# Tile 1's queries go straight behind the keys on SP's queue, and the values wait for a key transfer

## The chip, the cores and the metric

The kernel runs on one core of a Trainium2 chip. The metric is the device time of one execution in microseconds (us). A profiled execution also shows, per engine, when each instruction ran: PE is the matrix engine (PEld its weight loads), DVE, ACT and POOL are the engines that do element-wise work, and SP only issues DMA transfers. POOL and ACT issue DMA transfers as well. Each issuing engine has a DMA queue of its own: in the trace q0 is POOL's, q1 SP's and q10 ACT's.

## The reference

Attention over pooled keys and values, followed by a mixture of four experts in which every token uses every expert:

```python
# q, k, v: (8 batches, 8 heads, 576 tokens, 64), float32
k_p = k.reshape(B, H, S // 8, 8, D).mean(axis=3)      # 72 pooled keys
v_p = v.reshape(B, H, S // 8, 8, D).mean(axis=3)
scores = scale * np.matmul(q, k_p.transpose(0, 1, 3, 2))
attn = softmax(scores)
x = (attn @ v_p).transpose(0, 2, 1, 3).reshape(4608, 512)
p = domain_probs / (domain_probs.sum(-1, keepdims=True) + 1e-09)
out = sum(p[:, e:e+1] * (np.maximum(x @ w1[e], 0.0) @ w2[e] for e in range(4)))
```

w1 is (4, 512, 1024) and w2 is (4, 1024, 512). Nearly all products are those of the experts.

## The kernel before, in words

The 4608 tokens make 36 tiles of 128, and four tiles make a group. For each of the nine groups and each of the four experts PE computes h = relu(x w1) (`up`, L465, copied out by ACT at L469) and then the four tiles' outputs h w2 (`down`, L503, weighted and summed by DVE at L514 and L518). The attention of the next group is put between these products by a plan of slots that is written out by hand (L548 to L597). This steady part starts with the loop at L795.

The change lies in the part ahead of it (L134 to L207 and L600 to L792), which has to make the first group's x from nothing. Instructions stand on each engine in the order in which the code is written, and each engine works through its own in order. The dependencies between engines become semaphore waits, set when the program is built.

The loads at the start are spread over three queues:

- ACT's queue: the queries of tile 0 (`qf[0]`, L144).
- SP's queue: the first batch's keys as float32 in three transfers (`kf`: the 64 last rows at L147, then two times 256 rows at L149). Later, from inside the loop over key parts, the queries of tile 1 (`load_q0(1, nc.sync)`, L726, issued by L139) and the domain probabilities (`dpr`, L727).
- POOL's queue: first a copy of one element of `qf[0]` (L170), which makes POOL wait until those queries have landed. Behind it, in this order: the first batch's values in three transfers (`vraw[0]`, L81 two times, L85), the first half of `w1[0]` (L119), tile 2's queries, the second half of `w1[0]`, tile 3's queries, `w2[0]` in two halves (L127), `w1[1]`, and all that follows. POOL's transfers convert float32 to bfloat16, apart from the queries of tiles 2 and 3.

A transfer on POOL's queue waits, from the ninth on, for the landing of the one eight places before it.

The work on the engines then goes, from L715 on: idle products on PE (`idle_products`, products of zeros whose result is not used, L626); `split_q(0)` casts tile 0's queries on ACT (L601), `turn_q0` turns them on PE (L609), `take_q0` copies them out on ACT (L617). The loop at L721 takes the keys in three parts, in the order in which they are loaded: `fold_keys0` sums eight rows to one on DVE (L640 two times, L645), `turn_keys0` turns the sums on PE (L652), and a few idle products follow. Between the fold and the turning of the second part stand a memset of one element of `qf[1]` on DVE (L725) and the two SP transfers named above; the transfer into `qf[1]` overwrites that element, so SP waits for the memset, and the memset stands behind the folds on DVE. `take_keys0` copies the turned keys to SBUF in two halves of 64 partitions, both on DVE (L665).

After that come `scores(0)` (PE, L328), `split_q(1)`, `turn_q0(1)` and `take_q0(1)` for tile 1, the maxima, differences and exponentials of tile 0 (DVE L342 and L346, ACT L359), `sum_values0` (PE, L672: eight products for the first two row blocks, which need the first value transfer, and eight for the other three, which need the second and third) with `spread_values0` (DVE, L681), the scores of tile 1, and the rest of tile 0's attention: its transposes and their copy (L402, L403), the sums (L693), the context (L418) and its transposes (L707, L710). The first products with `w1[0]` follow (`up_tile`, L481), which from then on fill PE.

Of the kernel before, what the change touches and what calls it, by code (L numbers as in the profile page):

```python
# [18 lines left out]
def kernel(  # L19
# [10 lines left out]
    nc = tc.nc  # L30
# [3 lines left out]
    P = nc.NUM_PARTITIONS  # L34
# [43 lines left out]
    def load_rows(dst, src, parts=((0, NB - 1),)):  # L78
        rows = src.rearrange("h (j r) d -> (h j) (r d)", r=POOL)
        for i0, i1 in parts:  # L80
            nc.gpsimd.dma_start(  # L81
                out=dst[:, i0:i1, :],
                in_=rows[i0 * P:i1 * P].rearrange("(i p) x -> p i x", p=P),
            )
        nc.gpsimd.dma_start(out=dst[0:TAIL, NB - 1, :], in_=rows[(NB - 1) * P:ROWS])  # L85
# [50 lines left out]
    qf = [raw.tile([P, R, D], F32, name=f"qf{c}") for c in range(TPG)]  # L136

    def load_q0(c, queue):
        queue.dma_start(  # L139
            out=qf[c][:].rearrange("p r d -> p (r d)"),  # L140
            in_=q[0][:, c * P:(c + 1) * P, :].rearrange("h (c r) d -> c h (r d)", r=R),
        )

    load_q0(0, nc.scalar)  # L144
    kf = raw.tile([P, NB, POOL * D], F32, name="kf")
    rows0 = k[0].rearrange("h (j r) d -> (h j) (r d)", r=POOL)
    nc.sync.dma_start(out=kf[0:TAIL, NB - 1, :], in_=rows0[(NB - 1) * P:ROWS])  # L147
    for i in (0, 2):
        nc.sync.dma_start(  # L149
            out=kf[:, i:i + 2, :],  # L150
            in_=rows0[i * P:(i + 2) * P].rearrange("(i p) x -> p i x", p=P),
        )
    dpr = const.tile([NT, P, E], F32, name="dpr")

    still = const.tile([P, G], BF16, name="still")
    nc.vector.memset(still[:], 0.0)  # L156
# [5 lines left out]
    for sign, base in ((1, 0), (-1, SP - 1)):  # L162
        nc.gpsimd.affine_select(
            out=own[:], in_=own[:], compare_op=ALU.is_ge, fill=0.0,
# [2 lines left out]
        )  # L167

    waited = const.tile([1, 1], F32, name="waited")
    nc.gpsimd.tensor_copy(out=waited[:], in_=qf[0][0:1, 0, 0:1])  # L170
    load_rows(vraw[0], v[0], ((0, 2), (2, 4)))
    load_w1(0, lambda: load_q0(2, nc.gpsimd))
    load_q0(3, nc.gpsimd)
# [409 lines left out]
    for g in range(2, NG):  # L583
        for i in range(TPG):
            t = g * TPG + i
# [37 lines left out]
    def idle_products(n):  # L623
        ps = ps_o.tile([P, DM], F32, name="o_ps")
        for _ in range(n):
            nc.tensor.matmul(ps[:], lhsT=still[:, 0:P], rhs=still[:], start=True, stop=True)  # L626
# [8 lines left out]
    def fold_keys0(p1, i0, i1):  # L635
        rows = kraw[0][0:p1, i0:i1]
        src = kf[0:p1, i0:i1]
        for n in (4, 2):
            w = n * D
            nc.vector.tensor_add(  # L640
                out=rows[:, :, 0:w], in0=src[:, :, 0:w], in1=src[:, :, w:2 * w]
            )
            src = rows
        twice = [p1, i1 - i0, 2, D]
        nc.vector.tensor_tensor(  # L645
            out=kpad0[0:p1, i0:i1], in0=rows[:, :, 0:D].unsqueeze(2).to_broadcast(twice),
            in1=rows[:, :, D:2 * D].unsqueeze(2).to_broadcast(twice), op=ALU.add,
        )

    def turn_keys0(p1, i0, i1):  # L650
        for i in range(i0, i1):
            nc.tensor.transpose(  # L652
                kT_ps[:, i, 0:p1], kpad0[0:p1, i].rearrange("p z d -> p (z d)"),
                ident[0:p1, 0:p1],
            )

    def take_keys0():
        for z in range(2):
            dst, src = (
                x[z * D:(z + 1) * D].rearrange("x i p -> x (i p)")[:, 0:ROWS].rearrange(  # L660
                    "x (a y j) -> x a y j", y=2, j=SP
                )[:, :, z]
                for x in (kT[0], kT_ps)
            )
            nc.vector.tensor_copy(out=dst, in_=src)  # L665


    def sum_values0():
# [51 lines left out]
    take_q0(0, turn_q0(0))  # L720
    for part, n in (((TAIL, 4, 5), 3), ((P, 0, 2), 4), ((P, 2, 4), 3)):  # L721
        fold_keys0(*part)
        if part[2] == 2:

            nc.vector.memset(qf[1][0:1, 0, 0:1], 0.0)  # L725
            load_q0(1, nc.sync)  # L726
            nc.sync.dma_start(  # L727
                out=dpr[:], in_=moe_domain_probs.rearrange("(t p) e -> t p e", p=P)
            )
        turn_keys0(*part)  # L730
        idle_products(n)
    take_keys0()
    scores(0)
    split_q(1)
# [60 lines left out]
    for s in range(NSTEP):  # L795
        for slot in range(SLOTS):
            part, i = slot % 3, slot // 3
# [41 lines left out]
```

## Time and profile before

| | |
|---|---|
| median of 3 runs | 553.97 us (553.47 to 554.54) |
| profiled execution | 554.65 us |
| its span, first to last instruction | 552.7 us |
| PE busy | 542.3 us (98%) |
| DVE, ACT, POOL busy | 263.3, 212.7, 70.7 us |
| granted PE clock, mean | 0.993 |
| first product with `w1[0]` (L481) | 22.81 us |
| loop at L795 reached (L465) | 40.7 us |

Times in the profile count from the first instruction of the span. A row of the timeline or of the chain gives start, length, engine, line, what is written and read, and how many instructions it merges. A wait is given with the engine and line that waited and what ended the wait. "DMA to landing" is the time from a transfer's issue to the semaphore that tells that it is complete. A row of the table by windows gives, for each stretch, each engine's busy time with its number of instructions, then the granted PE clock as a share, the busy share of the DMA engines, and GB/s.

### The profile page before, as it was taken

The numbers are of one execution on the slowest core, as the hardware profiler recorded it, in microseconds if no ns is written. First come the engines' busy times: TensorE is split into PE (matmuls) and PEld (weight loads), VectorE is DVE, ScalarE is ACT, GpSimd is POOL, SyncE is SP. The second block draws the span as 40 slices with busy tenths as digits, with TensorE's granted clock in tenths as the row PEclk, the third lists the DMA queues.
The fourth block names the chain that finished last, engine by engine and source line by source line (L and its number), as shares of the span: only waits on it lengthen the run. The fifth ranks groups of instructions, "written<-read, shape, count | busy, mean of one in ns | idle before, by whom it ended". The sixth has DMA issues, their size and how long they took to land.

```text
span 552.7 us, 7479 instructions
## 1 busy us (share of the span) xinstructions
PE 542.3 (98%) x3000; PEld 264.3 (48%) x3000; DVE 263.3 (48%) x458; ACT 212.7 (38%) x356; POOL 70.7 (13%) x120
## 2 busy tenths in 40 slices
PE   6899999999999999999999999999999999999997
PEld 2674554444444444444444444444444444444444
DVE  5572857444744445644463444744474444422223
ACT  1465653333333333333333333333333333333330
POOL 6344001121101110112011100101010000000000
PEclk9799999999999999999999999999999999999999
DMA  9999925455646664356535653335333241011002
GB/s 205 223 203 197 200 33 99 73 78 82 119 85 79 83 105 96 54 83 84 106 52 73 85 117 40 53 40 98 61 53 42 72 77 31 16 44 39 0 1 76
DMA packets 110273, 46.43 MB, mean 84 GB/s; under 512 B 87548, under 2 KB 104764, under 8 KB 110240
## 3 DMA queue, kind: packets, MB, share of 16 engines
q0 software_dynamic: 51040, 21.96, 32.1%
q1 hardware_dynamic: 58912, 23.68, 18.0%
q8 instruction: 23, 0.38, 0.3%
q10 hardware_dynamic: 288, 0.33, 0.3%
q14 instruction: 10, 0.08, 0.0%
HBM read 45.16 MB, written 9.44 MB: 99 GB/s over the span
## 4 chain that ended last, share of the span: by engine, by line
PE 96%; DMA 2%; ACT 1%; DVE 0%; issue 0%; SPq 0%; ACTq 0%
PE o_ps L503 45%; PE h_ps L465 44%; PE x_ps L418 2%; PE sc L328 2%; PE h_ps L481 1%; DMA qf<-in_q_dram 1%; DMA kf<-in_k_dram 1%; PE x_ps L448 1%; PE v_ps L672 0%; PE at_ps L402 0%; PE o_ps L535 0%; ACT attnT L403 0%; PE qT_ps L318 0%; PE o_ps L626 0%; DVE kraw L640 0%; PE qT_ps L609 0%
## 5 line engine op out<-in xcount | busy, mean ns | idle before, releaser
L469 ACT ACTIVATE h_sb<-h_ps 128x512 bf16<-128x512 f32 x280 | 167.1, 597 | 296.2 <-PE h_ps L465 293.8
L465 PE MATMUL h_ps<-xT,w 128*128 128x512 bf16 x1120 | 274.1, 379 | 0.0
L503 PE MATMUL o_ps<-w,h_sb 128*128 128x512 bf16 x1144 | 270.3, 379 | 0.0
L503 PEld LDWEIGHTS <-h_sb 128*128 128x128 bf16 x1144 | 111.5, 98 | 132.7
L518 DVE SCALAR_TENSOR_TENSOR acc<-o_ps,p_sb,acc 128x512 f32<-128x512 f32 x107 | 80.3, 750 | 179.4 <-PE o_ps L503 179.4
L465 PEld LDWEIGHTS <-w 128*128 128x128 bf16 x1120 | 106.0, 98 | 117.1
L514 DVE TENSOR_SCALAR acc<-o_ps,p_sb 128x512 f32<-128x512 f32 x36 | 27.0, 750 | 62.3 <-PE o_ps L503 62.3
L561 POOL COPY gated<-x_sb0of 1x1 bf16<-1x1 bf16 x28 | 7.8, 278 | 369.8 <-DVE x_sb0of L427 369.8
L109 POOL DMA_DIRECT2D qrow<-in_q_dram x36 | 30.5, 847 | 23.7 <-issue 7.7
L342 DVE TENSOR_REDUCE mx<-sc 128x8 f32<-128x576 f32 x36 | 27.2, 756 | 11.5 <-PE sc L328 11.5
L346 DVE TENSOR_TENSOR d_sb<-sc,mx 128x576 f32<-128x576 f32 x36 | 27.3, 757 | 1.2
L427 DVE SCALAR_TENSOR_TENSOR x_sb0of<-x_ps,rs 128x512 bf16<-128x512 f32 (+1 forms) x30 | 20.2, 674 | 12.4 <-PE x_ps L418 11.7
L359 ACT ACTIVATE attn<-d_sb 128x576 bf16<-128x576 f32 x30 | 20.5, 683 | 3.2
L380 DVE TENSOR_REDUCE es<-attn 128x8 f32<-128x576 bf16 x28 | 20.8, 743 | 0.0
L418 PEld LDWEIGHTS <-attnT 128*128 128x128 bf16 (+1 forms) x165 | 12.4, 100 | 7.2 <-issue 1.3
L328 PEld LDWEIGHTS <-qT 128*128 128x128 bf16 (+1 forms) x160 | 11.3, 101 | 8.8 <-issue 2.0
L328 PE MATMUL sc<-kT,qT 128*128 128x144 bf16 (+1 forms) x160 | 15.3, 230 | 0.1
L418 PE MATMUL x_ps<-vbd,attnT 128*128 128x192 bf16 (+5 forms) x165 | 15.2, 231 | 0.0
L626 PE MATMUL o_ps<-still 128*128 128x512 bf16 x31 | 10.6, 473 | 1.3 <-DVE still L156 1.3
L243 DVE TENSOR_TENSOR vraw<-vraw 128x1280 bf16<-128x1280 bf16 (+1 forms) x14 | 9.2, 654 | 0.2
L243 DVE TENSOR_TENSOR kraw<-kraw 128x1280 bf16<-128x1280 bf16 (+1 forms) x14 | 9.0, 640 | 0.2
L481 PE MATMUL h_ps<-xT,w 128*128 128x128 bf16 x128 | 8.3, 219 | 0.3
(88 smaller groups left out, 155.4 us busy)
## 6 DMA issues: line engine op xcount, KB each, us to landing
out_dram<-acc SPq DMA_DIRECT2D x35, 256.0 KB, 2.0
w<-in_moe_w_dram POOLq DMA_DIRECT2D x10, 512.0 KB, 14.3
kraw<-in_k_dram POOLq DMA_DIRECT2D x7, 512.0 KB, 8.0
qrow<-in_q_dram POOLq DMA_DIRECT2D x28, 128.0 KB, 3.8
vraw<-in_v_dram POOLq DMA_DIRECT2D x7, 512.0 KB, 7.5
w<-in_moe_w_dram POOLq DMA_DIRECT2D x3, 1024.0 KB, 16.3
kf<-in_k_dram SPq DMA_DIRECT2D x2, 512.0 KB, 5.4
vraw<-in_v_dram POOLq DMA_DIRECT2D x2, 256.0 KB, 4.8
```

Of the source, the lines that this page charges most:

```text
L109: nc.gpsimd.dma_start(out=qrow[t][at:at + n], in_=q[b][:, tok:tok + n, :].rearrange("h p d -> p h d"),)
L328: nc.tensor.matmul(sc[at:at + n, pair // 2, (pair % 2) * PW:(pair % 2 + 1) * PW], lhsT=qT[t][:, pair, at:at + n], rhs=kT[b][:].rearrange(" ...
L342: nc.vector.reduce_max(out=mxs[t][:], in_=by_head(t), axis=AX.X)
L346: nc.vector.tensor_tensor(out=st[t][:], in0=by_head(t), in1=mxs[t][:].unsqueeze(3).to_broadcast([P, 2, 4, SP]), op=ALU.subtract,)
L359: nc.scalar.activation(out=attn[t % 2][:, 0:ROWS].rearrange("p (h j) -> p h j", j=SP), in_=st[t][:].rearrange("p g h j -> p (g h) j"), fun ...
L380: nc.vector.reduce_sum(out=es[:], in_=e, axis=AX.X)
L418: nc.tensor.matmul(ps[at:at + n, h0 * D:(h0 + c1 - c0) * D], lhsT=attnT[t][:, i, at:at + n], rhs=flat[:, c0 * D:c1 * D], start=(i == 0), s ...
L465: nc.tensor.matmul(ps[:], lhsT=w1_sb[e][:, kc, fb * P:(fb + 1) * P], rhs=xT[g][:, kc, :], start=(kc == 0), stop=(kc == KC - 1),)
L469: nc.scalar.activation(out=hs[s][:, fb, :], in_=ps[:], func=ACT.Relu)
L503: nc.tensor.matmul(ps[:], lhsT=hs[s][:, fb, i * P:(i + 1) * P], rhs=w2_sb[e][:, fb, :], start=(fb == 0), stop=(fb == FB - 1),)
L514: nc.vector.tensor_scalar_mul(out=accs[t][:], in0=ps[:], scalar1=p_sb[:, e, t:t + 1])
L518: nc.vector.scalar_tensor_tensor(out=accs[t][:], in0=ps[:], scalar=p_sb[:, e, t:t + 1], in1=accs[t][:], op0=ALU.mult, op1=ALU.add,)
```

## The change

Four edits. The transfer of tile 1's queries and that of the probabilities are issued on SP right behind the three key transfers, and the memset that they waited for is gone. POOL's copy of one element, ahead of the values, reads an element of the keys' second transfer (`kf`, row block 0) in place of one of tile 0's queries. The two halves of the turned keys are copied one on DVE and one on ACT.

```diff
@@ the loads on SP
             out=kf[:, i:i + 2, :],
             in_=rows0[i * P:(i + 2) * P].rearrange("(i p) x -> p i x", p=P),
         )
+    load_q0(1, nc.sync)
     dpr = const.tile([NT, P, E], F32, name="dpr")
+    nc.sync.dma_start(out=dpr[:], in_=moe_domain_probs.rearrange("(t p) e -> t p e", p=P))
@@ ahead of POOL's loads
     waited = const.tile([1, 1], F32, name="waited")
-    nc.gpsimd.tensor_copy(out=waited[:], in_=qf[0][0:1, 0, 0:1])
+    nc.gpsimd.tensor_copy(out=waited[:], in_=kf[0:1, 0, 0:1])
     load_rows(vraw[0], v[0], ((0, 2), (2, 4)))
@@ take_keys0
-            nc.vector.tensor_copy(out=dst, in_=src)
+            (nc.vector.tensor_copy, nc.scalar.copy)[z](out=dst, in_=src)
@@ the loop over the key parts
         fold_keys0(*part)
-        if part[2] == 2:
-
-            nc.vector.memset(qf[1][0:1, 0, 0:1], 0.0)
-            load_q0(1, nc.sync)
-            nc.sync.dma_start(
-                out=dpr[:], in_=moe_domain_probs.rearrange("(t p) e -> t p e", p=P)
-            )
         turn_keys0(*part)
         idle_products(n)
```

## The prediction

> **What bounds the kernel now.** I read the page first: PE is busy 542.3 of 552.7 us, and only the first two of the 40 slices show less than 9 tenths. From 40.85 us on the windows show PE busy throughout, so whatever this change is worth is decided before that, and a gain made there is kept unless a later load becomes late. Next the chain that ended last, in order of time (start, length, what):
>
> ```profile
> 7.86 0.05 DVE kraw L640
> 7.91 6.82 DMA qf<-in_q_dram
> ...
> 14.81 0.63 ACT qrow L601
> ...
> 15.48 0.64 PE qT_ps L609 x16
> ...
> 16.66 2.13 PE v_ps L672 x16
> 18.80 0.48 PE sc L328 x4
> 19.27 0.43 PE at_ps L402 x5
> ```
>
> The transfer of tile 1's queries sits on it for 6.82 us. The waits of PE and ACT up to 22 us, and SP's own, give its price and its cause:
>
> ```profile
> PE qT_ps L609 <- ACT qrow L601: 4.9, 1, 4.9
> ...
> ACT qrow L601 <- DMA qf<-in_q_dram: 9.2, 2, 7.1
> ...
> SPq L139 <- DVE kraw L640: 6.0, 1, 6.0
> ```
>
> PE stands still from 10.61 to 15.48 (4.88 us), and SP had nothing to issue from 2.52 to 7.91, waiting for the fold and the memset of L725. Then the DMA queues between issue and first packet, 8 to 11.9 us, and from 12 to 14.8 us (packets, MB, share):
>
> ```profile
> q0 software_dynamic: 743, 0.71, 119.9%
> ```
> ```profile
> q0 software_dynamic: 299, 0.46, 75.2%
> q1 hardware_dynamic: 188, 0.33, 37.1%
> ```
>
> In the first stretch SP's queue (q1) moved not one packet although its transfer had been issued at 7.91: it stood behind the POOL queue's (q0) values and weights. Last, the values:
>
> ```profile
> DMA to landing us min/median/max: 4.1/5.1/5.4
> ```
>
> Issued at 5.03, 5.86 and 6.57, they land at 9.1, 11.3 and 11.6: long before PE uses them at 16.45. And the clock, in windows whose edges I put on the clock record's steps (5.77, 12.60, 19.43) and halfway between:
>
> ```profile
> 9.19:12.60 3.41, 1.34 (x9) 0.64 (x9) 2.12 (x4) 0.00 (x0) 3.13 (x6) 1.00 1.18 190
> 12.60:16.01 3.41, 0.53 (x16) 0.51 (x16) 0.00 (x0) 0.62 (x1) 1.09 (x2) 0.50 1.14 263
> 16.01:19.43 3.42, 3.42 (x30) 3.03 (x26) 0.60 (x1) 1.17 (x2) 1.39 (x3) 0.50 1.21 245
> 19.43:22.84 3.41, 2.93 (x28) 1.77 (x27) 3.26 (x9) 1.42 (x4) 1.44 (x2) 1.00 1.23 205
> ```
>
> After the stretch with 1.34 us of PE work (first number in front of a bracket) the clock falls to 0.50, and it comes back only after a full one. So the idle time also slows the values' products behind it.
>
> **The change part by part.** Times are on the scale of the profiled execution.
>
> *Tile 1's queries and the probabilities on SP.* The DVE memset (0.06 us) goes, and with it SP's wait. The two issues (0.61 and 0.62 us) follow the last key issue, 2.5 to 3.8 us; nothing else stands on SP's queue until the transposes at 86 us. Their 0.26 and 0.07 MB go behind the keys. Alone, SP's queue moved 0.28 MB in the 0.80 us from 5.0 to 5.8, so they add 0.75 and 0.21 us to the keys' last packet at about 7.1 to 7.3: done at about 8.1. From last packet to landing took 0.45 to 1.0 us for keys and queries, so tile 1's queries land at 8.4 to 9.0 instead of 14.73. The keys stand ahead on the same queue; I take their landings (6.49, 7.77) as unchanged, with 1.0 us late, all of the new traffic, as the bad end.
>
> *The values' gate.* POOL's one-element copy now waits for the second key transfer (6.49) instead of tile 0's queries (4.86): 1.63 us. Behind it on POOL stand the values, both halves of w1[0], the queries of tiles 2 and 3, w2[0] and all later loads; each is issued up to 1.63 us later. The first value packet came at 6.64, 1.61 us behind its issue, and the first of them took about 0.5 us each until SP's queue was empty at 7.3. Now the first comes at 6.66 + 1.61 = 8.27, with SP's queue empty. The shift of the values is thus between 1.2 (counted from where they ran freely) and 1.63 us: last landing at 12.8 to 13.3. I take 13.0, since the freed DMA engines should return part. For later loads the 0.33 MB no longer come between: from 12 to 14.8 us q0 moved 299 packets, where its 743 in 3.9 us give 533, so 1.2 us were lost there and come back. Their net shift is 0 to 0.4, with 1.63 as the bad end.
>
> *The keys' copy on two engines.* Here the built program shows more than the diff: ACT's copy does not wait for PE but for DVE's semaphore at the value which the first half's copy sets. The two halves run one after the other. Before: 0.62 us for both on DVE from 9.52. Now 0.31, a hand-over of 0.05 (the gaps between DVE, ACT and PE in the chain are 0.02 to 0.06), and ACT's half: its copies took 0.325 at 128x256 and 0.69 at 128x640, so 0.36 at 288. End 10.24 instead of 10.14. Bounds: 0.25 earlier if side by side, 0.2 later with the slower hand-overs. ACT's next piece, the cast of tile 1's queries, also waits behind it, though its data are there at 9.0.
>
> *The sum.* Scores of tile 0 on PE 10.3 to 10.7; cast on ACT 10.26 to 10.88; turning on PE (0.44 as for tile 0) to 11.4; one idle product; the first eight value products (values landed by 10.7) to about 12.15. ACT's copy of the turned queries ends at 12.0; DVE's maxima and differences (0.76 each) end at 12.3, exponentials at 13.0. So PE waits from 12.15 for the last values: 13.05. The eight products with 192 columns took 1.28 of the 2.13 us at clock 0.50, so 0.64 at full: end 13.7 instead of 18.79. From there to the first product with w1[0] it was 4.02 us (22.81); 0.48 and 0.43 of it were scores and transposes at half clock, which take 0.26 and 0.29 at full (25.53 and 24.03 us in the chain): 3.66. That product then starts at 17.36: 5.45 us earlier; with values at 13.3 it is 5.15, at 12.8 it is 5.65, and if they never bound (PE free at 12.15) 6.3.
>
> Whether the weights are there: landings (issue plus time to landing) 15.1 and 18.3 for w1[0] against needs of 17.4 and 20.2 (25.62 before); tile 2's queries 16.2 against 18.1; w2[0] 21.5 and 24.6 against 24.2 and 25.5 (29.66 and 30.93 before). The last has the least cover, 0.9 us. Behind it w1[1] (27.2 against 35.3), the second batch's keys (32.6 against 34.4) and w2[2] (59.4 against 62.7; used at 68.05 before) stay covered. Nothing else moves, so I take 5.4 us. The profiled execution took 554.65 us, 1.95 around its span; less 5.4 it is 549.25. It lies 0.68 above the median 553.97, so for the median: 548.6.
>
> *Two rules beside the rows.* The trace: the clock fell at 12.60, after 2.0 us of idle PE, when the stretch before it held 1.34 us of work. The Trainium skill (TensorE: Matmul & The Clock Gate, "What's actually happening") says that the monitor watches free-running windows of about 3.4 us and gates after an idle one; the window length agrees with the steps here, but this window was not idle. By the rule 0.9 us of waiting could never bring half clock; by the row it could, so the rival below is kept. On the queues the row is the missing 4 us of SP packets. The Trainium skill (DMA: Bandwidth & Descriptors, "Queues, rings and completion order") has each DMA engine alternate between queues packet by packet; by that rule the 128 packets of tile 1's queries, at half of 190 per us from 9.3 on, would have landed by about 11.5 (an estimate), 3 us sooner than they did, and lifting the gate would bring 2.2 us instead of 5.4; the trace does not agree.
>
> **The rivals.**
>
> *Half clock stays.* From 9.19 to 12.60 PE would work about 2.5 us by my sum, between 1.34 (fell) and 2.93 (held), nearer the second. If it falls, the value products cost 0.64 more, scores and transposes 0.36, and one more stretch of sums, context and transposes about 1: gain 3.4, 550.6.
>
> *A weight comes late.* With the whole 1.63 us kept, the second half of w2[0] lands at 26.3 against 25.5: 0.8 lost, 549.4. For it: the DMA queue is full until 60 us. Against: the 1.2 us returned.
>
> *The keys come late,* because SP's queue shares its engines with what stands behind: 1.0 us on keys, gate and values: 549.6. Against: the same queue serves in order in the rows.
>
> *Hidden anyway, no change.* If tile 1's queries still wait until POOL's queue has drained, they land near 14 and PE waits as before: 554. Against: POOL now issues 4 us after SP.
>
> *Slower.* The values are held behind SP's queue as tile 1's queries were behind POOL's: first packet 4.07 us after issue instead of the 1.37 of the first keys, 2.7 lost. If each of the three value transfers lost that in turn, the last lands at 21.1, and the kernel is 2.7 us slower: 556.7. It decides from a landing later than 18.5. Against: before, the first value packets came 1.61 us after issue while SP's queue still ran.
>
> **How the numbers follow.** My forecast (values set the pace, 547.6 to 549.0): 0.62. Still better, to 547.2 (the values never bind and the key copies do run side by side): 0.04. Weight late 0.09, keys late 0.05, half clock 0.12: all faster. Hidden 0.03; slower 0.05. From no change a measurement can tell about 0.2%, 1.1 us. Faster 0.92, same 0.03, slower 0.05. The range from 547.2 to 550.8 reaches over the faster cases; what lies beyond is the last two, and some of the tails.
>
> **What would show it.** SP's four issues and the probabilities' without a pause before 4 us; tile 1's cast on ACT at about 10.3, ended by ACT's own copy and not by a DMA; ACT's key copy starting after DVE's; no 4.9 us wait on PE, but one of about 0.9 before L674's last eight products, ended by the values' DMA; a clock of 1.00 from 12.6 to 19.4; the first product with w1[0] near 17.4, and from there everything of before some 5.4 us sooner. Wrong would be: values landing after 14, half clock after 12.6, or a PE wait for w2[0] near 25.

## The result, and the profile after

The changed kernel takes 549.91 us (median of 6 runs, 549.07 to 550.60) against 554.02 us before (6 runs, 553.46 to 555.63). The ratio is 0.9923 with a 95% interval of 0.9907 to 0.9939: 0.6 to 0.9% faster. The forecast was 548.6, with a range from 547.2 to 550.8. The profiled execution took 549.99 us with a span of 547.9, which is 4.8 us less than the span of before. One run of the kernel with only the new gate (712.42 us, mean clock 0.754) and one of the kernel before beside it (637.78 us, 0.848) were slow ones and are left out of the medians below.

The chain that ended last in the changed kernel, in order of time (start, length, what). Lines behind L155 carry numbers 2 higher than before.

```profile
6.08 0.70 POOL waited L172
6.79 1.49 POOL vraw L81 x2
8.27 5.14 DMA vraw<-in_v_dram
...
13.46 0.83 PE v_ps L674 x8
14.29 0.25 PE sc L330 x4
```

Tile 1's queries are gone from it. In their place stand POOL's gate copy, the issue of the values, and the landing of the last of them. PE's waits up to 22 us say the same:

```profile
PE v_ps L674 <- DMA vraw<-in_v_dram: 1.5, 1, 1.5
...
PE qT_ps L611 <- ACT qrow L603: 0.2, 1, 0.2
```

The wait for the cast of tile 1's queries fell from 4.9 to 0.2 us, and one of 1.5 us for the values came. The timeline shows how each edit came out:

```profile
2.56 0.61 SPq L139 DMA_DIRECT2D qf<-in_q_dram  x1
...
3.21 0.59 SPq L155 DMA_DIRECT2D dpr<-in_moe_domain_probs_dram  x1
...
6.05 0.69 DVE L642 TENSOR_TENSOR kraw<-kf 128x512 bf16<-128x512 f32 x1 [1.56 <-DMA kf<-in_k_dram]
6.08 0.70 POOL L172 COPY waited<-kf 1x1 f32<-1x1 f32 x1 [4.00 <-DMA kf<-in_k_dram]
...
9.33 0.30 DVE L667 COPY kT<-kT_ps 64x288 bf16<-64x288 bf16 x1 [0.38 <-PE kT_ps L654]
...
9.66 0.39 ACT L667 COPY kT<-kT_ps 64x288 bf16<-64x288 bf16 x1 [2.45 <-DVE kT L667]
...
10.08 0.62 ACT L603 CAST qrow<-qf 128x512 bf16<-128x512 f32 x1
...
17.94 1.27 PE L483 MATMUL h_ps<-xT,w 128*128 128x128 bf16 x16
```

SP issues without a pause. Tile 1's queries took 6.2 us from issue to landing and were there at 8.8; their cast follows ACT's own copy and waits for no transfer. The two halves of the keys run one after the other: ACT waited for DVE. The first product with `w1[0]` comes at 17.94 instead of 22.81. From there to the end everything is as long as before: from the loop's first product (L465, now L467) to the end of the span it is 512.0 us in both.

One row shows something new. POOL's copy of one element, 0.18 us before, took 0.70, ending with the DVE instruction beside it.

And the clock stayed at 1.00 from its first step, at 4.85 us, on. Counted from that step, the stretch of 3.41 us that had least PE work in it was this one:

```profile
11.68:15.09 3.41, 1.91 (x24) 1.41 (x21) 1.18 (x3) 1.05 (x3) 2.78 (x4) 1.00 1.17 189
```

### The profile page after: what moved, and what is told of

Read it like the earlier page. It is cut to its first block, busy times and chain, and to the rows that moved or that the text cites. A ratio compares the mean times of both kernels' runs of the same rounds, so it can differ in the third digit from the quotient of the medians.

```text
span 547.9 us, 7477 instructions
## 1 busy us (share of the span) xinstructions
PE 540.3 (99%) x3000; PEld 262.3 (48%) x3000; DVE 262.9 (48%) x456; ACT 213.3 (39%) x357; POOL 71.2 (13%) x120
## 4 chain that ended last, share of the span: by engine, by line
PE 96%; DMA 2%; ACT 1%; POOL 0%; DVE 0%; issue 0%; SPq 0%
PE o_ps L505 45%; PE h_ps L467 44%; PE x_ps L420 2%; PE sc L330 2%; PE h_ps L483 1%; DMA vraw<-in_v_dram 1%; DMA kf<-in_k_dram 1%; PE x_ps L450 1%; PE at_ps L404 0%; PE o_ps L537 0%; POOL vraw L81 0%; ACT attnT L405 0%; PE qT_ps L320 0%; ACT xT L712 0%; PE v_ps L674 0%; POOL waited L172 0%
## 5 line engine op out<-in xcount | busy, mean ns | idle before, releaser
L467 PE MATMUL h_ps<-xT,w 128*128 128x512 bf16 x1120 | 274.2, 379 | 0.0
L467 PEld LDWEIGHTS <-w 128*128 128x128 bf16 x1120 | 105.8, 98 | 117.2
L348 DVE TENSOR_TENSOR d_sb<-sc,mx 128x576 f32<-128x576 f32 x36 | 27.3, 757 | 1.2
## 6 DMA issues: line engine op xcount, KB each, us to landing
w<-in_moe_w_dram POOLq DMA_DIRECT2D x10, 512.0 KB, 14.2
kraw<-in_k_dram POOLq DMA_DIRECT2D x7, 512.0 KB, 6.4
vraw<-in_v_dram POOLq DMA_DIRECT2D x7, 512.0 KB, 5.9
kf<-in_k_dram SPq DMA_DIRECT2D x2, 512.0 KB, 5.0
```

What stands on the lines that cost most here:

```text
L348: nc.vector.tensor_tensor(out=st[t][:], in0=by_head(t), in1=mxs[t][:].unsqueeze(3).to_broadcast([P, 2, 4, SP]), op=ALU.subtract,)
L467: nc.tensor.matmul(ps[:], lhsT=w1_sb[e][:, kc, fb * P:(fb + 1) * P], rhs=xT[g][:, kc, :], start=(kc == 0), stop=(kc == KC - 1),)
```

## The experiments

### How much of the gain is the clock

The kernel before, with PE kept busy during the wait; no transfer is moved.

```diff
     take_keys0()
     scores(0)
+    idle_products(20)
     split_q(1)
```

> The kernel before with 20 more idle products behind the scores of tile 0, some 4.3 us of PE work in the wait for tile 1's queries; no transfer is moved. My theory: the clock stays at 1.00 past 12.6 us, the queries land at 14.7 as before, and what stands behind them up to the first product with w1[0] is 1.0 to 1.5 us shorter; 552.5 to 553.2. The rest of the change's gain is the transfer's. Rival (the clock is most of the gain): 551 or less. Third outcome (the clock falls all the same): 554.0.

Measured: 552.34 us (552.27 to 552.93), ratio 0.9970 (0.9959 to 0.9981). All six runs had a mean clock of 1.000, where 12 runs of the kernel before beside them had 0.994 to 0.997. The chain:

```profile
7.84 7.06 DMA qf<-in_q_dram
...
15.65 0.44 PE qT_ps L609 x14
16.09 0.33 PE o_ps L626
16.41 1.11 PE v_ps L672 x16
```

The transfer still takes 7 us, and landed at 14.89, 0.16 later than before. Behind it the value products take 1.11 us instead of 2.13, and the first product with `w1[0]` comes at 21.17 instead of 22.81. The clock alone is worth 1.9 us by the medians, a little more than the 1.0 to 1.5 expected for it. The rival, that it is most of the gain, falls: 1.9 of 4.1 us.

### The parts of the change one by one

The first run has only the SP edit; the second puts it together with the two-engine copy, without the new gate; the third has the SP edit and the new gate, without the two-engine copy; the fourth has only the new gate.

The changed kernel with the old gate and both copies on DVE, that is, the kernel before with only the SP transfers moved:

```diff
-    nc.gpsimd.tensor_copy(out=waited[:], in_=kf[0:1, 0, 0:1])
+    nc.gpsimd.tensor_copy(out=waited[:], in_=qf[0][0:1, 0, 0:1])
...
-            (nc.vector.tensor_copy, nc.scalar.copy)[z](out=dst, in_=src)
+            nc.vector.tensor_copy(out=dst, in_=src)
```

> The kernel before with only the two SP transfers put behind the keys and the memset gone. My theory: this edit alone carries the gain; it is as fast as the changed kernel with the old gate, 549.1 (548.6 to 549.9). Rival (the three edits are needed together): 550.5 or more.

Measured: 548.75 us (548.53 to 549.52), ratio 0.9901 (0.9886 to 0.9916). Repeated on another occasion:

> Only the two SP transfers moved, once more: 548.4 to 549.5 as before (548.75), clock 1.00 in all runs, third key transfer at about 7.8 us. If it comes out over 549.6, its lead of 1.1 us over the changed kernel was of the occasion.

Measured: 549.02 us (548.41 to 549.34), ratio 0.9905 (0.9891 to 0.9919); the third key transfer landed at 8.3 here, at 7.8 in the first. So the SP edit alone carries the gain and more: its ten runs lie between 548.41 and 549.52, the changed kernel's six between 549.07 and 550.60. By the medians the SP edit alone is 0.9 to 1.2 us below the changed kernel, though measured on other occasions. Its chain has no transfer behind the keys any more:

```profile
2.06 5.71 DMA kf<-in_k_dram
...
7.79 0.70 DVE kraw L642
...
10.19 0.42 PE sc L330 x4
...
10.64 0.77 DVE mx L344
...
11.43 0.77 DVE d_sb L348
...
12.22 0.69 ACT attn L361
```

The values, issued at 4.95, land at 11.63, and the second eight products start at 11.68 with no wait. From the third key part on it is the work itself that follows: fold, scores, maxima, differences, exponentials.

The changed kernel with only the gate put back:

```diff
-    nc.gpsimd.tensor_copy(out=waited[:], in_=kf[0:1, 0, 0:1])
+    nc.gpsimd.tensor_copy(out=waited[:], in_=qf[0][0:1, 0, 0:1])
```

> The changed kernel with the values' gate put back on tile 0's queries. My theory (since the change, the landing of the last values sets the pace, one for one): the values are issued at about 5.0 us and land at 11.6 to 12.3, PE is ready for them at about 12.1, the first product with w1[0] comes at 17.0 to 17.3 instead of 17.94; about 0.8 us faster than the changed kernel, 549.1. Rival (the gate earns its place because the values would hold up the keys): the third key transfer lands 0.7 us or more later than 7.6, PE is ready later by as much, and the kernel is no faster than the changed one: 549.9 or more.

Measured: 549.32 us (548.79 to 549.69), ratio 0.9909 (0.9894 to 0.9924). The median is 0.6 below the changed kernel's, where the theory had 0.8, and the ranges overlap. The values land at 12.53, the first product with `w1[0]` comes at 17.06. Both theories had a point: the third key transfer landed at 8.1 instead of 7.6. But the SP edit alone also has the old gate, and its keys landed at 7.8 and 8.3; with the new gate and both copies on DVE (next) they landed at 8.4. A difference of 0.5 us and more is thus from execution to execution.

The changed kernel with both copies on DVE:

```diff
-            (nc.vector.tensor_copy, nc.scalar.copy)[z](out=dst, in_=src)
+            nc.vector.tensor_copy(out=dst, in_=src)
```

> The changed kernel with both halves of the turned keys copied on DVE as before. My theory: PE waits 1.5 us for the values behind this copy, so nothing is seen at the end: within 0.2 us of the changed kernel, 549.9, scores of tile 0 within 0.15 us of 10.10. Rival (the copy on ACT carries part of the gain): 0.3 us or more slower, 550.2.

Measured: 549.86 us (549.29 to 550.12), ratio 0.9918 (0.9904 to 0.9931): the same time as the changed kernel. The scores of tile 0 came at 10.83, not within 0.15 us of 10.10 as I had said, because the third key transfer landed at 8.4 in this execution; that is no effect of the copy, which comes later. Nor did PE wait 1.5 us for the values here. They were issued as in the changed kernel (6.70 against 6.73) but landed at 12.48 instead of 13.41, and the first product with `w1[0]` came at 17.18. The chain that ended last runs through another load behind the gate, the second half of `w2[0]`:

```profile
12.15 13.38 DMA w<-in_moe_w_dram
...
25.58 1.02 PE o_ps L505 x4
```

So this run does not show that the wait for the values hides the copy. By the times the two-engine copy does nothing that can be measured; beside the old gate its median is 0.3 to 0.6 us higher (549.32 against 548.75 and 549.02), with ranges that overlap.

The kernel before with only the new gate:

```diff
-    nc.gpsimd.tensor_copy(out=waited[:], in_=qf[0][0:1, 0, 0:1])
+    nc.gpsimd.tensor_copy(out=waited[:], in_=kf[0:1, 0, 0:1])
```

> The kernel before with only the values' gate on the second key transfer. My theory: tile 1's queries are still issued at 7.9 us and still set the pace, though POOL's queue is less full by then, so they land 0 to 1.5 us earlier: 552.6 to 554.2, PE waiting 3.5 us or more for the cast of tile 1's queries. Rival (the later gate gives the gain, by emptying the queue for them): they land before 11.5 and the kernel takes 551 or less.

Measured: 551.44 us (median of five runs, 550.28 to 551.74; ratio 0.9942, 0.9925 to 0.9960), between what either theory gave: tile 1's queries landed at 11.87, 2.9 us earlier than before, and still set the pace. The DMA queues from 8 to 11.9 us (packets, MB, share):

```profile
q0 software_dynamic: 494, 0.49, 79.7%
q1 hardware_dynamic: 145, 0.26, 19.8%
```

In the same stretch of the kernel before q1 had no packet at all. The queries were issued at 7.47, only 0.7 us behind the first value transfer, and got through; before, they were issued 2.9 us behind it, and waited until 12. So the new gate does part of what the SP edit does, in another way, and the two do not add up. Against the medians of before beside them, the SP edit brought 5.6 and 5.3 us, the gate alone 2.9, and both together 4.5 (copies on DVE) and 4.1 (the changed kernel).

### Do the values set the pace

The changed kernel with the gate on the third key transfer.

```diff
-    nc.gpsimd.tensor_copy(out=waited[:], in_=kf[0:1, 0, 0:1])
+    nc.gpsimd.tensor_copy(out=waited[:], in_=kf[0:1, 2, 0:1])
```

> The changed kernel with the values' gate on the third key transfer, which lands at 7.6 in place of 6.0. My theory (the last values set the pace, one for one): the values are issued 0.9 to 1.6 us later than 6.73 and land as much later than 13.4; the first product with w1[0] moves by the same, 550.9 to 551.5, up to 1 us more if the clock falls in the longer wait. Rival (something else is due at the same time, so that the slope is under a half): 550.4 or less.

Measured: 551.36 us (551.13 to 552.45), ratio 0.9954 (0.9939 to 0.9968), 1.45 us above the changed kernel. The chain:

```profile
7.77 0.70 POOL waited L172
8.48 1.49 POOL vraw L81 x2
9.96 4.82 DMA vraw<-in_v_dram
...
14.82 1.16 PE v_ps L674 x8
```

The values land 1.37 us later (14.78), and the median moves by 1.45: one for one. But the gate holds the weights too: the second half of `w2[0]` landed at 27.43, 1.42 us later. Its first product came at 28.55 in this execution; in the three runs that were 1.1 to 1.3 us shorter it was due at about 27.3 (an estimate), as early as the weight landed. The run thus shows what the gate costs, one for one, but does not tell the values from that weight. This execution, one of the two at 552.45 with a mean clock of 0.997, also lost the clock from 15.18 to 18.60; the other three, at 551.13 to 551.36, had 0.999 or 1.000.

### What holds POOL's copy

First another engine does the waiting: ACT writes one element of the values' tile, which the first value transfer overwrites and therefore waits for.

```diff
-    waited = const.tile([1, 1], F32, name="waited")
-    nc.gpsimd.tensor_copy(out=waited[:], in_=kf[0:1, 0, 0:1])
+    qrow[0] = qpool.tile([P, R, D], BF16, name="qrow")
+    nc.scalar.copy(out=qrow[0][:], in_=qf[0][:])
+    nc.scalar.copy(out=vraw[0][0:1, 0, 0:1], in_=kf[0:1, 0, 0:1])
     load_rows(vraw[0], v[0], ((0, 2), (2, 4)))
...
-    split_q(0)
```

> The changed kernel in which not POOL but ACT waits for the second key transfer and writes one element into the values' tile, which the value transfer then waits for. POOL's copy took 0.70 us in the changed kernel, just as long as DVE's fold beside it, and 0.18 before with DVE idle. My theory (POOL's copy is held by DVE's fold): the values are issued about 0.45 us earlier behind the keys' landing, 0.25 to 0.35 us after it instead of 0.70, and land as much earlier: 549.4 to 549.7. Rival (the issue of the transfer itself is what DVE holds up): it still starts 0.7 us after the landing: 549.9.

Measured: 549.51 us (549.30 to 550.80), ratio 0.9922 (0.9906 to 0.9937): the median lies where the theory had it, but the intervals don't tell it from the changed kernel. The trace does show a shorter way: ACT's copy at 6.00 takes 0.19 us and the values are issued at 6.51, 0.53 us behind the keys' landing (5.98), not 0.70 us (6.03 to 6.73). That is 0.17 us, not the 0.35 to 0.45 expected, as a hand-over of about 0.3 us from ACT to POOL took its place. The values landed at 12.44, no earlier than the 12.48 with POOL's copy and both key copies on DVE. The first product with `w1[0]` came at 16.98, 0.96 us before the changed kernel's, but only 0.5 us of that was left at the end, since PE then waited for the second half of `w2[0]` (landed at 25.54; L506 is L503 of before):

```profile
PE o_ps L506 <- DMA w<-in_moe_w_dram: 0.3, 1, 0.3
```

The run at 550.80 had a mean clock of 0.996; the three others had 1.000.

Then a DVE that is busy with something else: the kernel with only the SP transfers moved (old gate), and four sums on tiles of their own, whose results nobody uses.

```diff
+    side = const.tile([P, 2, G], F32, name="side")
+    sum_of = const.tile([P, G], BF16, name="sum_of")
+    nc.vector.memset(side[:], 0.0)
     make_mask_v()
+    for _ in range(4):
+        nc.vector.tensor_add(out=sum_of[:], in0=side[:, 0], in1=side[:, 1])
     split_q(0)
```

> Only the two SP transfers moved, old gate; DVE also does four sums of 512 columns from float32 to bfloat16 on tiles of its own (results unused), each of the fold's form, so that it is busy from about 3.9 to 6.7 us, when POOL's gate copy comes at about 4.9. My theory (a DVE instruction of this form holds up POOL's copy whatever it reads): the copy takes 0.3 to 0.7 us or more instead of 0.18, ending with one of DVE's sums. Rival (the copy was slow because it read the tile that DVE read): 0.18 us. The folds come about 1 us later in either case, so the time says nothing here.

One run was taken, 550.00 us. The timeline of DVE and POOL:

```profile
3.67 2.87 DVE L724 TENSOR_TENSOR sum_of<-side 128x512 bf16<-128x512 f32 x4
```
```profile
4.66 0.46 POOL L172 COPY waited<-qf 1x1 f32<-1x1 f32 x1 [2.58 <-DMA qf<-in_q_dram]
```

The four sums take 0.72 us each, so the second ends at 5.10; POOL's copy, started at 4.66, ends at 5.12. It took 0.46 us, where the same copy took 0.18 with DVE idle. It reads another tile than DVE, so the shared tile is not the cause: the copy waits for the end of the DVE instruction beside it. The loop's own one-element copies by POOL (`gated`, L561 of the kernel before) agree: most of the 28 take 0.18 us, and one at 91.8 us, beside a two-input sum on DVE, takes 0.71. POOL's issue of transfers is not held in this way: the first two value transfers took 1.55 us to issue before, after and here. The Trainium skill (SBUF — State Buffer, "Who interferes with whom") says that a DVE instruction with two inputs in SBUF contends with a POOL instruction that reads SBUF, because its second input comes through a read port that the two share. These runs agree: 0.70 and 0.46 against 0.18 us. No run here has the copy beside a DVE instruction with one input, so that part is not shown.

### Does the gate protect the keys

No gate for the values at all, on the kernel with only the SP transfers moved:

```diff
     waited = const.tile([1, 1], F32, name="waited")
-    nc.gpsimd.tensor_copy(out=waited[:], in_=qf[0][0:1, 0, 0:1])
     load_rows(vraw[0], v[0], ((0, 2), (2, 4)))
```

> Only the two SP transfers moved and no gate at all for the values, both key copies on DVE. My theory (values beside the keys take their share of the engines): values issued at about 2.2 us, the second and third key transfers land 1.0 to 2.0 us later than 6.0 and 7.8, so that PE comes to the scores of tile 0 that much later than 10.2, while the values land at about 9: 549.5 to 550.8, worse than with the old gate (548.75). Rival (the keys keep their place, being issued first): 548.0 to 548.7.

Measured: 548.57 us (548.10 to 551.45), ratio 0.9907 (0.9889 to 0.9926). By the times the rival is right: no gate is as fast as the old one. But the execution that the profile shows is the one at 551.45, and for the keys it is as my theory had it (the values landed at 11.76, not at about 9): third key transfer at 9.57, scores of tile 0 at 11.99, clock down from 12.79 to 16.20. The stretch ahead of that step:

```profile
9.38:12.79 3.41, 1.73 (x26) 1.06 (x27) 2.24 (x6) 0.62 (x1) 1.80 (x3) 1.00 1.23 206
```

I then filled that stretch with PE work, 8 idle products more behind the second key part:

```diff
-    for part, n in (((TAIL, 4, 5), 3), ((P, 0, 2), 4), ((P, 2, 4), 3)):
+    for part, n in (((TAIL, 4, 5), 3), ((P, 0, 2), 12), ((P, 2, 4), 3)):
```

> The kernel without any values' gate, with 12 instead of 4 idle products behind the second key part, so that the stretch of 3.41 us ahead of 12.8 us is more than half full of PE work. My theory (a stretch with less than about 1.8 us of PE work makes the clock fall): no run with a clock under 0.999, no run over 549.2; median 548.2 to 548.7. Rival (the idle products delay the third key part's turning, or the clock falls for another reason): a run of 550 or more, or a median over 549.

Measured: 550.28 us (549.32 to 550.61), ratio 0.9925 (0.9904 to 0.9945), all clocks 1.000. The clock held, as the theory had it, but the median is 1.7 us worse, as the rival had it. In the profiled execution the idle products delay nothing: they end at about 10.7, and the third key part's sums are ready at 11.3. To see which of the two was the exception, the kernel without a gate once more:

> The kernel without a values' gate once more, beside the one with only the SP transfers moved. If the later end with 12 idle products (550.28 against 548.57) came of the idle products: 548.1 to 548.9 again in most runs, near the other kernel. If it came of the keys, whose landing beside ungated values differs from one occasion to the next: third key transfer at 9.5 us or later and 549.3 to 550.6 here.

Measured: 548.58 us (548.05 to 551.37), ratio 0.9899 (0.9883 to 0.9914). Again the profiled execution is the longest (551.37, third key transfer at 9.55, clock down from 12.53), and the four others lie at 548.05 to 548.81. So the kernel without a gate has the keys' delay in both of its profiled executions and cannot have all of it in the others. If the keys land earlier there, 12 idle products get in their way, which would fit the 1.7 us. That is argued, not shown: no trace of the others exists. What stands is that no gate and the old gate cannot be told apart by their medians (548.57 and 548.58 against 548.75 and 549.02).

## Why the prediction was right, and where it was off

The mechanism was right in its steps as the profiled execution shows them. The wait of PE for tile 1's queries went; the values took its place on the chain, with 1.5 us of waiting; the two-engine copy was serial and brought nothing. The late gate showed that the gate's delay counts one for one. That it is the values that set the pace is shown for the profiled executions of the changed kernel and of the late gate only; with both copies on DVE, and with ACT's gate, it was a weight. The SP edit alone brought 5.3 to 5.6 us, near the 5.4 forecast for the whole.

Tile 1's queries landed at 8.79 (said: 8.4 to 9.0). The keys landed at 6.03 and 7.58, not later for the 0.33 MB behind them in this execution. In the seven others that have these transfers and some gate the third key transfer landed between 7.6 and 9.0, in the three without them between 7.4 and 7.8, so some delay of the keys (a rival with 0.05) is not excluded. The scores of tile 0 came at 10.10 (10.3), and from the end of the value products to the first product with `w1[0]` it was 3.65 us (3.66).

The gain came out smaller, 4.1 instead of 5.4 us. Of this 0.6 us was in the sum, as the profiled execution has it. The term that was mis-sized is **the values' gate**: the last values landed at 13.41, not at 13.0, and outside the 12.8 to 13.3 given. I had charged the later release and nothing else. The keys even landed 0.46 us earlier than in the trace of before. But POOL's copy, which I had let stand at 0.18 us, took 0.70 beside the fold that the same landing starts, so the values were issued at 6.73 all the same. From there the transfers took 3.8 to 5.5 us to landing, as long as before (4.1 to 5.4): in this execution the freed DMA engines returned nothing. That differs from one execution to the next: with both copies on DVE they took 3.8 to 4.6 us behind the same gate. The value products took 0.83 us for eight, not 0.64. Most of the remaining 0.7 us is in how I went from one execution to a median: the profiled execution before lay 0.6 to 0.7 us above its median, the one after 0.1 above, and I carried the first offset over as if it belonged to the kernel. The other 0.2 us is the time around the span, 2.1 us instead of 1.95.

The net shift of later loads was mis-sized too, and hidden. I said 0 to 0.4 us with 1.63 as the bad end. The halves of `w1[0]` landed 1.0 and 2.1 us later than before (16.06 and 20.40), those of `w2[0]` 2.0 and 1.4 (23.47 and 26.01). The second half of `w1[0]` was first used at 20.81 and that of `w2[0]` at 26.11, so the rival "a weight comes late" missed by 0.4 and 0.1 us. Here one miss covered another, which is luck: had the values landed 0.4 us earlier, as forecast, the product at 26.11 would have had to wait for its weight. With both copies on DVE and with ACT's gate it did: the values landed at 12.48 and 12.44, the weight at 25.54, and the profiled executions took 549.51 and 549.39 us, near the 549.4 that the rival gave. A PE wait for `w2[0]` near 25 us was one of the signs named for being wrong; it is in those two traces and not in the changed kernel's. Moving the gate cost about 1 us in all, between the SP edit with the new gate (549.86) and with the old one (548.75).

The rival of the clock was also nearer than its 0.12 suggests. I had 2.5 us of PE work from 9.19 to 12.60 (it was 2.37), but I had taken the steps of the trace before for granted. They lie elsewhere in each execution: the first was at 5.77 us before, at 4.85 after, at 3.98 with both copies on DVE. At its own steps the changed kernel's weakest stretch had 1.91 us; steps at other places would have met a weaker one:

```profile
10.00:13.41 3.41, 1.62 (x29) 1.10 (x28) 1.51 (x2) 1.94 (x4) 3.07 (x6) 1.00 1.13 168
```

All six runs kept the clock (mean 0.999 or 1.000); by the rows that follow, that owes something to luck. The stretches ahead of a fall, in executions of three experiments (gate alone, late gate, no gate; the last one's row stands above), were these:

```profile
9.69:13.10 3.41, 1.10 (x22) 0.65 (x21) 1.75 (x3) 0.62 (x1) 3.30 (x5) 1.00 1.16 232
```
```profile
11.77:15.18 3.41, 0.96 (x13) 0.79 (x13) 0.47 (x1) 0.88 (x2) 3.40 (x6) 1.00 1.16 175
```

Over all profiled executions of this study, up to 40 us, the clock fell from 1.00 after stretches with 0.96, 1.10, 1.34 (before), 1.49 and 1.73 us of PE work in 3.41, and held after every one with 1.91 (the changed kernel), 2.08 or more. The Trainium skill (TensorE: Matmul & The Clock Gate, "What's actually happening") has the clock fall after an idle window. The runs agree with its windows, not with the word idle: these five stretches were 28 to 51% full, and it turned somewhere near half.

## What to carry to other kernels

When a transfer on one queue waits for a long time on the chain, look at what another queue had put on the DMA engines ahead of it: issuing it earlier was worth 5.3 to 5.6 us here, and letting the others in later 2.9, but the two are one gain, and the second has its price on everything behind the gate, weights included. A gate should be no heavier than its wait: one element copied by POOL took 0.70 us instead of 0.18, because the same landing starts a two-input DVE instruction beside it. And a PE wait can cost its length and then the clock behind it: here waits of 1.9 to 4.9 us were followed by half clock, and one of 1.5 was not. So count the PE work in stretches of 3.41 us, wherever these may start, when you predict what a shorter wait is worth.

## What was not expected of the hardware

POOL's one-element copy is held until the end of a DVE sum that runs beside it (0.70 and 0.46 us against 0.18). How much SP's transfer got in between POOL's went with when it was issued: from 8 to 11.9 us it moved 145 packets when issued 0.7 us behind the first value transfer (gate alone), 56 at 2.3 us (the kernel kept warm) and none at 2.9 us (before); what decides it stays open. And a kernel whose keys and values compete for the DMA engines had 2.5 to 3.4 us more in both of its profiled executions than in nine of its others (548.05 to 548.84), so one profile was not typical of its runs there.
